# Slot logits in column groups by token tile, with a running maximum and total in each group

## The chip, the cores and the metric

The program runs on one core of one Trainium2 chip. A core has engines that run side by side and meet at semaphores: TensorE (PE in the profile), which multiplies matrices and writes to PSUM, eight banks of 128 partitions x 512 fp32 columns; its weight loader (PEld); VectorE (DVE), ScalarE (ACT) and GpSimd (POOL), which work on PSUM and on SBUF; and SyncE (SP), which issues most transfers (DMA) from and to HBM. The metric is device time in microseconds (us) of one execution, as the median of several runs; lower is better.

## The reference

Three stages in a row, all fp32, on 2304 tokens of width 512. The first is attention with random features (exponentials of projections in place of a softmax), the second a mixture of four experts (`relu(x @ w1[e]) @ w2[e]`, weighted by probabilities that are given). The change lies in the third, a mixture through slots; `x` is the second stage's output, `phi` is 512 x 32:

```
logits = x @ phi                                  # 2304 tokens x 32 slots
d = softmax of logits over the tokens (axis 0)
slot_input = d.T @ x                              # 32 slots x 512
slot_out[e] = relu(slot_input[e] @ w1[e]) @ w2[e] # 8 experts of 4 slots, inner width 1024
c = softmax of logits over the slots (axis 1)
out = c @ slot_out                                # 2304 x 512
```

The first softmax needs the maximum and the total over all tokens, before `slot_input` is final, and every slot waits for all tokens. The kernel does it as a running softmax: each group of tokens is scaled by the maximum so far, and what was summed before is corrected by the factor f = exp(old maximum - new maximum).

## The kernel before

The second stage is the longest. Each product of 128x384 tiles is three matmuls of high and low parts, and the blocks are combined so that seven products do the work of eight. The tokens lie in three buffers `x2[0..2]` of 768 tokens, features on the partitions, four blocks k of 128 features. The last seven second-layer products of the last unit (each 12 matmuls, L784) are P1 to P7 in a string `ENDING` (L841), which is written by hand and gives the order in which the program's pieces are emitted, and so the order on each engine: each engine runs its own instructions in that order and waits at semaphores. Between the products the string puts the first slot tasks; the digit is the group of tokens:

```
"l0 P1 l1 t0 P2 t1 l2 b0 P6 a0 t2 l3 b1 P5 a1 t3 g0 P3 b2 a2 l4 g1 P7 b3 a3 t4 g2 P4 b4 a4 g3"
```

There are NB = 6 groups of three tiles of 128 tokens. For each:

- l, `slot_logits`: four matmuls 32x384 (L956), one for each feature block k. The 32 slots fill only 32 of the array's 128 columns, so block k goes to column group k: partitions 32k to 32k+31 of the PSUM tile `lq` hold the part that block k gives. ScalarE copies `lq` to SBUF (L960; VectorE in the last group).
- t, `slot_sum`: one matmul with `sumr` (L966), a 128x128 matrix of four by four identities of 32, adds the four parts and leaves the sum `lt` on all four groups of partitions. VectorE takes the negative maximum (L974) and the smaller of it and the old one (L975), ScalarE writes the exponentials and their row totals (L978 and the read of the accumulator behind it), copies the plain logits (L981), and computes f (L987).
- b, `slot_back`: three transposes (L1007) of 64 rows, 32 of exponentials and 32 of plain logits, put tokens on the partitions; VectorE copies both out (L1015, L1012).
- a, `slot_turns`: for each tile four transposes of `x` into one bank `tpm` (L943 is the line of the transposes in the profile) and a copy of 128x512 to SBUF (L945).
- g, `slot_gather`: d.T @ x, three matmuls 32x512 (L1025), tile i in column group i, so three partial sums lie below one another in `acc`; VectorE adds them to the running sum, scaled by f (L1036), and brings the total up to date (L994).

PSUM tiles of these tasks take turns in the four banks of the group "s": a fifth tile has to wait until the first has been read for the last time.

What follows the string is the tail: logits, turns, sum and back of the last group, with the gather of the one before. `slots_turn` (L1100) then multiplies the running sum, 96 partitions, with `sf` (`sumr` times f, L1094): that adds the three partial sums and puts features on the partitions (`tps`), and a second time for the last group's own sum, which is first copied out (L1107, L1108). L1111 copies `tps` to `sp`, and `hidden` (L1160) starts the slots' first layer, `second_layer` (L1188) the second. The weights of these layers are 32 tiles of 1 MB; the loop at L1147 issues them from SyncE, and those whose place in SBUF is still in use wait there for the last reader.

Of the kernel before, what the change touches and what calls it, by code (L numbers as in the profile page):

```python
# [16 lines left out]
P = 128  # L17
# [20 lines left out]
NB = NT // NP  # L38
# [7 lines left out]
def body(ctx: ExitStack, tc: tile.TileContext, ql, kl, vl, om, dp, wl, phi, w2l, out):  # L46
# [786 lines left out]
    def widen():  # L833
# [8 lines left out]
        "l0 P1 l1 t0 P2 t1 l2 b0 P6 a0 t2 l3 b1 P5 a1 t3 g0 P3 b2 a2 l4 g1 P7 b3 a3 t4 g2 P4 b4 a4 g3"  # L842
# [68 lines left out]
    def begin_keep():  # L911
        nonlocal keep, lgs
        keep = prep.tile([P, NT + 2 * NP, NS], F32, name="keep", tag="prb0")
        lgs = keep[:, 0:NT]

    keep = lgs = None
# [4 lines left out]
    def slot_task(s):  # L921
        {"l": slot_logits, "t": slot_sum, "a": slot_turns, "b": slot_back, "g": slot_gather}[s[0]](int(s[1]))
# [3 lines left out]
    def spare_place(n):  # L926
        if n not in places:
            if n < 6:
                t = w1e.tile([P, 6, DM], F32, name="mo", tag="w1x")
                places.update({k: t[:, k] for k in range(6)})  # L930
            else:
                tag = ("u1", "u2", "s1", "s2", "u4", "r22")[n - 6]
                places[n] = lt.tile([P, DM], F32, name=f"sp_{tag}", tag=tag)
        return places[n]

    mo = spare_place

    def slot_turn(n, i):
        b, c0 = n // 2, (n % 2) * TH + i * P
        x = spare_place(4 + (n % 2) * 3 + i)  # L940
        tp = bank("s", "tpm").rearrange("p (k t) -> p k t", k=NK)
        for k in range(NK):
            nc.tensor.transpose(tp[:, k, :], x2[b][:, k, c0:c0 + P], ident)  # L943
        copy = nc.vector.tensor_copy if n == NB - 1 and i == 1 else nc.scalar.copy
        copy(out=x, in_=tp.rearrange("p k t -> p (k t)"))  # L945
        st["x2t", n, i] = x

    def slot_turns(n):
        for i in range(NP):
            slot_turn(n, i)  # L950

    def slot_logits(b):
        c0 = (b % 2) * TH
        lq = bank("s", "lq")[:, 0:TH]
        for k in range(NK):
            nc.tensor.matmul(  # L956
                lq[32 * k:32 * k + 32, :], lhsT=phis[:, k, :], rhs=x2[b // 2][:, k, c0:c0 + TH], start=True, stop=True,
            )
        st["lq", b] = mo(1 + 2 * (b % 2))
        (nc.vector.tensor_copy if b == NB - 1 else nc.scalar.copy)(out=st["lq", b][:, 0:TH], in_=lq)  # L960

    def slot_sum(n):

        w = TH
        lt = bank("s", "lt")[:, 0:w]
        nc.tensor.matmul(  # L966
            lt, lhsT=sumr.rearrange("p j s -> p (j s)"), rhs=st["lq", n][:, 0:w], start=True, stop=True
        )
        m, old = mrun[n % 2], mrun[(n + 1) % 2]
        if n == 0:  # L970
            nc.vector.tensor_reduce(out=m, in_=lt, axis=AX.X, op=ALU.max, negate=True)
        else:
            mt = mp.tile([P, 1], F32, name="mt", tag="mt")
            nc.vector.tensor_reduce(out=mt, in_=lt, axis=AX.X, op=ALU.max, negate=True)  # L974
            nc.vector.tensor_tensor(out=m, in0=mt, in1=old, op=ALU.min)  # L975
        st["dt", n] = mo(10) if n % 2 else mo(2)
        ds = tot if n == 0 else mp.tile([P, 1], F32, name="ds", tag="ds", bufs=3)
        nc.scalar.activation(out=st["dt", n][:, 0:w], in_=lt, func=AF.Exp, bias=m, scale=1.0, accum_out=ds)  # L978
        def as_they_are():

            nc.scalar.copy(out=st["dt", n][NS:2 * NS, 0:w], in_=lt[NS:2 * NS])  # L981

        if n < NB - 1:
            as_they_are()
        if n:
            st["f", n] = mp.tile([P, 1], F32, name="f", tag="f", bufs=3)
            nc.scalar.activation(out=st["f", n], in_=old, func=AF.Exp, bias=m, scale=-1.0)  # L987
        if n == NB - 1:
            as_they_are()
        st["ds", n] = ds  # L990

    def slot_total(n):
        if n:
            nc.vector.scalar_tensor_tensor(  # L994
                out=tot, in0=tot, scalar=st["f", n], in1=st["ds", n], op0=ALU.mult, op1=ALU.add
            )

    def slot_back(b):

        nt = NP  # L1000
        d = st["d", b] = keep[:, NT + NP * (b % 2):NT + NP * (b % 2) + NP]
        st["lg", b] = lgs[:, NP * b:NP * b + NP]
        tp = bank("s", "dp")[:, 0:nt * 2 * NS].rearrange("p (i a s) -> p i a s", a=2, s=NS)
        def back(a0, a1):
            r = slice(a0 * NS, a1 * NS)
            for i in range(nt):
                nc.tensor.transpose(  # L1007
                    tp[:, i, a0:a1, :].rearrange("p a s -> p (a s)"), st["dt", b][r, i * P:(i + 1) * P], ident[r, r]
                )

        def logits():
            nc.vector.tensor_copy(out=st["lg", b][:, 0:nt, :], in_=tp[:, :, 1, :])  # L1012

        back(0, 2 if b < NB - 1 else 1)
        nc.vector.tensor_copy(out=d[:, 0:nt, :], in_=tp[:, :, 0, :])  # L1015
        if b < NB - 1:
            logits()
        else:
            st["rest"] = lambda: (back(1, 2), logits())

    def slot_gather1(b):

        acc = bank("s", "acc")
        for i in range(NP):
            nc.tensor.matmul(  # L1025
                acc[32 * i:32 * i + 32, :], lhsT=st["d", b][:, i, :], rhs=st["x2t", b, i], start=True, stop=True,
            )
        return acc[0:NS * NP]

    def slot_gather2(b, acc):  # L1030
        s1 = mo(0)[0:NS * NP]
        if b == 0:
            nc.gpsimd.memset(mo(0)[NS * NP:P], 0.0)
            nc.vector.tensor_copy(out=s1, in_=acc)
        else:
            nc.vector.scalar_tensor_tensor(  # L1036
                out=s1, in0=s1, scalar=st["f", b][0:NS * NP], in1=acc, op0=ALU.mult, op1=ALU.add
            )
        slot_total(b)

    def slot_gather(b):
        slot_gather2(b, slot_gather1(b))
# [43 lines left out]
    nc.gpsimd.memset(s2[NS * NP:P], 0.0)  # L1086
    slot_logits(n)
    slot_turn(n, 0)
    slot_turn(n, 1)
    slot_sum(n)  # L1090
    slot_gather(n - 1)
    slot_turn(n, 2)
    sf = mp.tile([P, NS], F32, name="sf")
    nc.vector.tensor_scalar_mul(sf, sumr[:, 0, :], st["f", n])  # L1094
    slot_back(n)
# [9 lines left out]
    slots_turn(0, mo(0), sf)  # L1105
    acc = slot_gather1(n)
    nc.scalar.copy(out=s2[0:NS * NP, 0:HD], in_=acc[:, 0:HD])  # L1107
    nc.vector.tensor_copy(out=s2[0:NS * NP, HD:DM], in_=acc[:, HD:DM])  # L1108
    slots_turn(1, s2, sumr[:, 0, :])
    st["rest"]()  # L1110
    nc.scalar.copy(out=sp, in_=tp)  # L1111
    slot_total(n)
    nc.vector.tensor_scalar_add(tot, tot, 1e-9)
    nc.vector.reciprocal(out=rtot, in_=tot)
# [213 lines left out]
```

## Time and profile before

| | |
|---|---|
| median of three runs | 958.35 us (957.3 to 959.7) |
| profiled execution | 953.06 us |
| span of its trace | 951.3 us |
| TensorE busy | 932.7 us, 98% of the span |
| VectorE, ScalarE, GpSimd busy | 79%, 45%, 37% |
| first logits matmul of the third stage (L956) | 856.3 us into the span |
| first matmul of the slots' first layer (L1160) | 901.07 us |

The span runs from the first to the last instruction of the trace; the rest of an execution's time, 1.76 us here, lies around it. "Busy" sums an engine's instructions over the span. A view by windows cuts the span into stretches and gives for each engine its busy time, the number of instructions, the clock that TensorE was granted (1.00 is full) and the share of the transfer engines in use. The chain of waits goes back from the last instruction: at each step to what released it, or to the instruction before it on the same engine; what is on it set the end. In the rows, an fp32 matmul of the program appears as two records, so that four matmuls of 128x32 are x8.

### The profile page before, as it was taken

Reading aid. Unit: us, or ns where it says so; the run is one execution under the profiler, and the core shown is the slowest. Engines: PE = TensorE matmul, PEld = TensorE weight load, DVE = VectorE, ACT = ScalarE, POOL = GpSimd, SP = SyncE. Lnnn points to the kernel's source line nnn. Section 1 sums busy time; section 2 is a strip of 40 time slices with the busy share of each in tenths; the row PEclk is TensorE's granted clock in tenths of the full one; section 3 lists DMA queues with packets and bytes.
Section 4 is the critical chain, followed back from the end, with each engine's and each line's share of the span. In section 5 each row is a group of like instructions: output and inputs, shape, how many; then the busy total and the mean of one; then the engine's idle time right before and its main releaser. Section 6 shows DMA issues by size and latency. Waiting matters only on the chain.

```text
span 951.3 us, 15807 instructions
## 1 busy us (share of the span) xinstructions
PE 932.7 (98%) x6065; PEld 888.9 (93%) x6065; DVE 752.3 (79%) x1134; ACT 428.5 (45%) x841; POOL 353.7 (37%) x290
## 2 busy tenths in 40 slices
PE   8999999999999999999999999999999999999997
PEld 7999989999999999999999999999999999997544
DVE  7788885999998878888888888788888888876432
ACT  4899885335543334334244334343342433325322
POOL 7877872432452341434043423414250534000000
PEclk9999999999999999999999999999999999999998
DMA  7678767684968776887767666767667677747897
GB/s 254 220 238 308 246 219 238 193 300 140 350 219 298 242 244 210 303 264 256 247 212 243 211 230 206 253 212 251 210 228 239 216 249 223 272 154 287 354 419 284
DMA packets 82111, 236.51 MB, mean 249 GB/s; under 512 B 8749, under 2 KB 36597, under 8 KB 77941
## 3 DMA queue, kind: packets, MB, share of 16 engines
q1 hardware_dynamic: 78292, 225.29, 69.2%
q10 hardware_dynamic: 3744, 10.23, 2.8%
q8 instruction: 48, 0.79, 0.3%
q14 instruction: 27, 0.21, 0.1%
HBM read 211.86 MB, written 23.63 MB: 248 GB/s over the span
## 4 chain that ended last, share of the span: by engine, by line
PE 86%; DVE 6%; DMA 3%; ACT 2%; issue 1%; SPq 0%; ACTq 0%; DVEq 0%
PE X L608 19%; PE X L784 18%; PE B L608 15%; PE B L784 14%; PE kv L221 3%; PE num L245 3%; PE pj L177 2%; PE so L1188 2%; PE tp L235 2%; PE pj L178 2%; PE pj L179 2%; PE hq L1160 1%; DMA raw<-kl 1%; DVE x L806 1%; DMA x<-xt 1%
## 5 line engine op out<-in xcount | busy, mean ns | idle before, releaser
L806 DVE TENSOR_TENSOR x<-X,x 128x768 f32<-128x768 f32 x84 | 80.0, 952 | 42.0 <-PE X L784 42.0
L419 POOL TENSOR_TENSOR Tw<-raww 128x512 f32<-128x512 f32 x30 | 41.3, 1397 | 192.5 <-DMA raww<-wl 192.5
L608 PE MATMUL X<-x,w1h 128*128 128x384 f32 x432 | 110.2, 335 | 0.2 <-PE B L784 0.2
L608 PE MATMUL B<-x,w1h 128*128 128x384 f32 x432 | 109.9, 335 | 0.0
L608 PE MATMUL X<-x,w1x 128*128 128x384 f32 x504 | 94.2, 334 | 0.6 <-DMA x<-xt 0.6
L608 PEld LDWEIGHTS X<-x,w1x 128*128 128x128 f32 x504 | 87.9, 188 | 0.9 <-ACT u L690 0.9
L202 ACT ACTIVATE fe<-pj,nb 128x128 f32<-128x128 f32 x288 | 82.7, 390 | 8.3 <-DVE nb L195 6.6
L655 ACT CAST s3h<-X 128x768 fp32r<-128x768 f32 x21 | 16.8, 802 | 147.7 <-DVE X L665 138.4
L608 PEld LDWEIGHTS X<-x,w1h 128*128 128x128 f32 x432 | 77.6, 188 | 0.8 <-PE B L784 0.5
L608 PEld LDWEIGHTS B<-x,w1h 128*128 128x128 f32 x432 | 77.8, 188 | 0.0
L608 PE MATMUL B<-x,w1l 128*128 128x384 f32 x216 | 72.2, 334 | 0.0
L608 PE MATMUL X<-x,w1l 128*128 128x384 f32 x216 | 72.2, 334 | 0.0
L806 DVE TENSOR_TENSOR x<-B,x 128x768 f32<-128x768 f32 x72 | 68.3, 949 | 3.3 <-PE B L784 2.8
L438 POOL TENSOR_TENSOR w2l<-raww,w2h 128x512 fp32r<-128x512 f32 x24 | 37.1, 1560 | 80.1 <-ACT w2h L437 80.1
L679 ACT COPY u<-X 128x768 f32<-128x768 f32 x63 | 50.1, 795 | 23.8 <-PE X L608 23.6
L185 DVE TENSOR_REDUCE stat<-pj 128x4 f32<-128x512 f32 x72 | 49.5, 687 | 12.7 <-PE pj L179 11.9
L438 POOL TENSOR_TENSOR w2l<-Tw,w2h 128x512 fp32r<-128x512 f32 x32 | 46.5, 1464 | 30.0 <-ACT w2h L437 30.0
L152 POOL TENSOR_TENSOR lo<-raw,hi 128x512 fp32r<-128x512 f32 x35 | 44.7, 1276 | 21.3 <-ACT hi L149 20.6
L438 POOL TENSOR_TENSOR w1l<-raww,w1h 128x512 fp32r<-128x512 f32 x25 | 38.0, 1524 | 36.6 <-ACT w1h L437 36.6
L655 ACT CAST e11h<-B 128x768 fp32r<-128x768 f32 x21 | 16.8, 801 | 77.0 <-PE B L784 68.5
L438 POOL TENSOR_TENSOR w1x<-Tw,w1x 128x512 fp32r<-128x512 f32 x21 | 27.7, 1317 | 57.4 <-ACT w1x L437 57.4
L608 PE MATMUL B<-x,w1x 128*128 128x384 f32 x252 | 47.1, 334 | 0.2 <-DMA x<-xt 0.2
(260 smaller groups left out, 2749.6 us busy)
## 6 DMA issues: line engine op xcount, KB each, us to landing
x<-xt SPq DMA_DIRECT2D x84, 768.0 KB, 5.3
x<-xd SPq DMA_DIRECT2D x75, 768.0 KB, 4.7
raww<-wl SPq DMA_DIRECT2D x16, 1024.0 KB, 6.8
w2tb<-w2l SPq DMA_DIRECT2D x11, 1024.0 KB, 9.6
raw<-ql SPq DMA_DIRECT2D x18, 512.0 KB, 5.0
xd<-xst SPq DMA_DIRECT2D x36, 256.0 KB, 3.0
prb<-prd SPq DMA_DIRECT2D x23, 384.0 KB, 6.6
raw<-kl SPq DMA_DIRECT2D x16, 512.0 KB, 5.8
```

Source lines behind the costliest of these rows:

```text
L152: (nc.gpsimd if i else nc.vector).tensor_tensor(out=lo, in0=r, in1=f32(hi), op=ALU.subtract)
L185: nc.vector.tensor_reduce(out=stats(i)[:, 4 * g:4 * g + 4, 0], in_=pjs[i, g], axis=AX.X, op=ALU.max)
L202: nc.scalar.activation(out=feats[i][:, 4 * g + h, :], in_=pjs[i, g][:, h, :], func=AF.Exp, bias=biases[i, g][:, h:h + 1], scale=1.0,)
L221: nc.tensor.matmul(kvps[b][h // 4][:, h % 4, :], lhsT=feats[i][p0:p0 + np_, h, :], rhs=v[p0:p0 + np_, h, :], start=first and h % 4 == 0, s ...
L245: nc.tensor.matmul(num[p0:p0 + n, h, :], lhsT=fts[i][:, 4 * g + h, p0:p0 + n], rhs=kvt[b][:, 4 * g + h, :], start=True, stop=True,)
L419: nc.gpsimd.tensor_tensor(out=out_, in0=a, in1=b_, op=op)
L438: nc.gpsimd.tensor_tensor(out=lo, in0=src, in1=f32(hi), op=ALU.subtract)
L608: nc.tensor.matmul(o, lhsT=lhs[:, jp, c], rhs=rhs[:, :, k, :], start=first and not k and not n, stop=False, skip_group_check=True,)
L655: nc.scalar.copy(out=pair(hs[i][0]), in_=src)
L679: nc.scalar.copy(out=pair(tmp({I1: "u1", I6: "u2", I5: "u4"}[i])), in_=q)
L784: nc.tensor.matmul(q[:, c, :], lhsT=lhs[:, jp, cs], rhs=rhs[:, jp, :], start=i in (I1, I2, I7) and jp == 0 and m == 0, stop=False, skip_gr ...
L806: nc.vector.tensor_tensor(out=o, in0=q, in1=o, op=ALU.add)
```

## The change

The tokens are now cut in five groups, `TG`: three of four tiles and two of three. The logits are laid out by tile, not by feature block: tile i of the group has column group i, and its four feature blocks are added up in PSUM in that column group (`start` at the first, `stop` at the last). So `lq` is 128 partitions (tile and slot) x 128 tokens and holds finished logits; the copy to SBUF and the matmul with `sumr`, task t, are gone. Each column group keeps a running maximum and total of its own (`mrun` and `tot` are 128 different values now, before they were four copies of 32). Exponentials and plain logits are both 128x128, and slot_back turns each with one transpose of 128x128. The gather is as before, with four tiles beside each other.

In the tail the four column groups are joined. `apart` spreads the 128 maxima over four columns by a mask, `slots_across` multiplies these with `sumr`, so that each partition sees the four groups' values of its slot, and takes the minimum of the negative maxima (`low`); w = exp(the group's own maximum minus the largest of the four) weights the groups: `s4w` is `sumr` times w, and times f for what was summed before, and `slots_turn` uses it in place of `sf` and `sumr`. The totals are weighted and added by a second `apart` and `slots_across`.

A cut of the diff, unchanged and removed lines left out where they are many:

```diff
...
-NB = NT // NP
+TG = [(0, 4), (4, 4), (8, 4), (12, 3), (15, 3)]
+NB = len(TG)
...
     ENDING = (
-        "l0 P1 l1 t0 P2 t1 l2 b0 P6 a0 t2 l3 b1 P5 a1 t3 g0 P3 b2 a2 l4 g1 P7 b3 a3 t4 g2 P4 b4 a4 g3"
+        "l0 P1 l1 P2 b0 P6 a0 b1 P5 g0 l2 a1 P3 g1 b2 P7 l3 a2 P4 g2 b3 a3"
...
     def begin_keep():
...
+        nonlocal lgs
+        lgs = prep.tile([P, NT, NS], F32, name="lgs", tag="prb0")
+        nc.gpsimd.memset(small(0, 4), 0.0)
+        for i in range(4):
+            nc.gpsimd.memset(small(i, 1)[32 * i:32 * i + 32], 1.0)
+    lgs = None
     tot = mp.tile([P, 1], F32, name="tot")
...
-        {"l": slot_logits, "t": slot_sum, "a": slot_turns, "b": slot_back, "g": slot_gather}[s[0]](int(s[1]))
+        {"l": slot_logits, "a": slot_turns, "b": slot_back, "g": slot_gather}[s[0]](int(s[1]))
     places = {}
...
-                tag = ("u1", "u2", "s1", "s2", "u4", "r22")[n - 6]
+                tag = ("u1", "u2", "u4", "s1", "s2", "r22")[n - 6]
                 places[n] = lt.tile([P, DM], F32, name=f"sp_{tag}", tag=tag)
...
+    def small(c, n):
+        return mo(2)[:, 384 + c:384 + c + n]
+    def slot_tile(n, i):
+        b, r = divmod(TG[n][0] + i, TB)
+        return x2[b], slice(r * P, (r + 1) * P)
     def slot_turn(n, i):
-        b, c0 = n // 2, (n % 2) * TH + i * P
-        x = spare_place(4 + (n % 2) * 3 + i)
+        x = spare_place(3 + 4 * (n % 2) + i)
         tp = bank("s", "tpm").rearrange("p (k t) -> p k t", k=NK)
+        y, c = slot_tile(n, i)
         for k in range(NK):
-            nc.tensor.transpose(tp[:, k, :], x2[b][:, k, c0:c0 + P], ident)
+            nc.tensor.transpose(tp[:, k, :], y[:, k, c], ident)
         copy = nc.vector.tensor_copy if n == NB - 1 and i == 1 else nc.scalar.copy
         copy(out=x, in_=tp.rearrange("p k t -> p (k t)"))
         st["x2t", n, i] = x
     def slot_turns(n):
-        for i in range(NP):
+        for i in range(TG[n][1]):
             slot_turn(n, i)
...
+    def rows(n):
+        return slice(0, NS * TG[n][1])
+    def slot_logits(n):
+        lq = bank("s", "lq")[:, 0:P]
         for k in range(NK):
...
+            for i in range(TG[n][1]):
+                y, c = slot_tile(n, i)
+                nc.tensor.matmul(
+                    lq[32 * i:32 * i + 32, :], lhsT=phis[:, k, :], rhs=y[:, k, c], start=k == 0, stop=k == NK - 1,
+                )
+        r = rows(n)
         m, old = mrun[n % 2], mrun[(n + 1) % 2]
         if n == 0:
-            nc.vector.tensor_reduce(out=m, in_=lt, axis=AX.X, op=ALU.max, negate=True)
+            nc.vector.tensor_reduce(out=m, in_=lq, axis=AX.X, op=ALU.max, negate=True)
         else:
             mt = mp.tile([P, 1], F32, name="mt", tag="mt")
...
+            nc.vector.tensor_reduce(out=mt[r], in_=lq[r], axis=AX.X, op=ALU.max, negate=True)
+            nc.vector.tensor_tensor(out=m[r], in0=mt[r], in1=old[r], op=ALU.min)
+        dt = st["dt", n] = mo(1 + n % 2)
         ds = tot if n == 0 else mp.tile([P, 1], F32, name="ds", tag="ds", bufs=3)
...
+        nc.scalar.activation(out=dt[r, 0:P], in_=lq[r], func=AF.Exp, bias=m[r], scale=1.0, accum_out=ds[r])
         if n:
...
+            f = st["f", n] = mp.tile([P, 1], F32, name="f", tag="f", bufs=3)
+            if n == NB - 1:
+                nc.gpsimd.memset(f[r.stop:P], 1.0)
+            nc.scalar.activation(out=f[r], in_=old[r], func=AF.Exp, bias=m[r], scale=-1.0)
+        nc.scalar.copy(out=dt[r, P:2 * P], in_=lq[r])
         st["ds", n] = ds
     def slot_total(n):
         if n:
+            r = rows(n)
             nc.vector.scalar_tensor_tensor(
-                out=tot, in0=tot, scalar=st["f", n], in1=st["ds", n], op0=ALU.mult, op1=ALU.add
+                out=tot[r], in0=tot[r], scalar=st["f", n][r], in1=st["ds", n][r], op0=ALU.mult, op1=ALU.add
             )
...
+    def slot_back(n):
+        r = rows(n)
+        t0, nt = TG[n]
+        dt = st["dt", n]
+        st["d", n] = dt[:, 2 * P:3 * P].rearrange("p (i s) -> p i s", s=NS)
+        def back(tp, *parts):
+            for a in parts:
+                nc.tensor.transpose(tp[:, a * P:a * P + r.stop], dt[r, a * P:(a + 1) * P], ident[r, r])
+        def logits(tp):
+            nc.vector.tensor_copy(
+                out=lgs[:, t0:t0 + nt, :], in_=tp[:, P:P + r.stop].rearrange("p (i s) -> p i s", s=NS)
+            )
+        def rest():
+            tp = bank("s", "dp")
+            back(tp, 1)
+            logits(tp)
+        tp = bank("s", "dp")
+        back(tp, *((0, 1) if n < NB - 1 else (0,)))
+        nc.vector.tensor_copy(out=dt[:, 2 * P:2 * P + r.stop], in_=tp[:, r])
+        if n < NB - 1:
+            logits(tp)
         else:
...
+            st["rest"] = rest
+    def slot_gather1(n):
...
-    def slot_gather(b):
-        slot_gather2(b, slot_gather1(b))
+        slot_total(n)
+    def slot_gather(n):
+        slot_gather2(n, slot_gather1(n))
+    def apart(c, v):
+        nc.vector.tensor_scalar_mul(small(c, 4), small(0, 4), v)
+    def slots_across(c, op):
+        a = bank("s", "across")[:, 0:4]
+        nc.tensor.matmul(a, lhsT=sumr.rearrange("p j s -> p (j s)"), rhs=small(c, 4), start=True, stop=True)
+        nc.vector.tensor_reduce(out=small(c + 4, 1), in_=a, axis=AX.X, op=op)
+        return small(c + 4, 1)
     def slot_shares():
         mx = mp.tile([P, NT, 1], F32, name="cmx")
     groups.update({"aq": [4], "bq": [5], "a": [2, 3, 0], "b": [1, 4], "c": [5, 6], "d": [7]})
     n = NB - 1
     s2 = mo(11)
-    nc.gpsimd.memset(s2[NS * NP:P], 0.0)
+    nc.gpsimd.memset(s2[rows(n).stop:P], 0.0)
     slot_logits(n)
+    last = mrun[n % 2]
+    apart(8, last)
+    slot_gather(n - 1)
+    low = slots_across(8, ALU.min)
+    w = small(16, 1)
+    nc.scalar.activation(out=w, in_=last, func=AF.Exp, bias=low, scale=-1.0)
+    s4w = mp.tile([P, 2, NS], F32, name="s4w")
+    nc.vector.tensor_scalar_mul(s4w[:, 1, :], sumr[:, 0, :], w)
+    nc.vector.tensor_scalar_mul(s4w[:, 0, :], s4w[:, 1, :], st["f", n])
     slot_turn(n, 0)
     slot_turn(n, 1)
-    slot_sum(n)
-    slot_gather(n - 1)
+    slot_back(n)
     slot_turn(n, 2)
...
+    slot_total(n)
+    nc.vector.tensor_tensor(out=small(17, 1), in0=tot, in1=w, op=ALU.mult)
+    apart(20, small(17, 1))
     tp = bank("bq", "tps")[:, 0:NK * NS].rearrange("p (k s) -> p k s", k=NK)
-    def slots_turn(m, lhs, rhs):
+    def slots_turn(m, lhs):
         for k in range(NK):
             nc.tensor.matmul(
-                tp[:, k, :], lhsT=lhs[:, k * P:(k + 1) * P], rhs=rhs,
+                tp[:, k, :], lhsT=lhs[:, k * P:(k + 1) * P], rhs=s4w[:, m, :],
                 start=m == 0 and k == 0, stop=m == 1, skip_group_check=True,
             )
-    slots_turn(0, mo(0), sf)
+    slots_turn(0, mo(0))
     acc = slot_gather1(n)
...
+    nc.scalar.copy(out=s2[rows(n), 0:HD], in_=acc[:, 0:HD])
+    nc.vector.tensor_copy(out=s2[rows(n), HD:DM], in_=acc[:, HD:DM])
+    total = slots_across(20, ALU.add)
     st["rest"]()
+    slots_turn(1, s2)
     nc.scalar.copy(out=sp, in_=tp)
...
+    nc.vector.tensor_scalar_add(rtot, total, 1e-9)
+    nc.vector.reciprocal(out=rtot, in_=rtot)
     slot_shares()
     for free in (mp, x2p, lt, w2p, hp, w1e, xop, w1p):
```

TensorE, between the first products. In before the logits (lq) of a group are followed, a few pieces later, by their sum (lt), and then by the turn back (dp); tpm are the turns of x, X the expert's product, acc the gather:

```order
L943 MATMUL tpm<-ident,x_0_2996 128x128 x12
L966 MATMUL lt<-mo,sumr 128x384
L956 MATMUL lq<-x_1_3276,phis 32x384 x4
L1007 MATMUL dp<-ident,sp_u_9248 128x64 x3
L784 MATMUL X_9197<-s1h,w2h 128x384
...
L943 MATMUL tpm<-ident,x_0_2996 128x128 x12
L966 MATMUL lt<-mo,sumr 128x384
L1025 MATMUL acc<-mo,keep 32x512 x2
L1025 MATMUL acc<-sp_u_9295,keep 32x512
L784 MATMUL X_9197<-s4h,w2h 128x384
```

After, in the same place:

```order
L953 MATMUL tpm<-ident,x_0_2996 128x128 x16
L1007 MATMUL dp<-ident,mo 128x128 x2
L785 MATMUL X_9216<-s1h,w2h 128x384
...
L1031 MATMUL acc<-mo 32x512 x3
L1031 MATMUL acc<-sp_u_9316,mo 32x512
L970 MATMUL lq<-x_1_3276,phis 32x128 x16
L953 MATMUL tpm<-ident,x_0_2996 128x128 x8
L953 MATMUL tpm<-ident,x_1_3276 128x128 x8
L785 MATMUL X_9216<-s4h,w2h 128x384
```

The lt rows are gone, a logits row counts sixteen matmuls of 128 columns in place of four of 384, a run of turns is four tiles long, and the turn back is two transposes in place of three.

TensorE in the tail, from the last group's logits to the first layer (hq), before:

```order
L956 MATMUL lq<-x_2_3576,phis 32x384 x4
L943 MATMUL tpm<-ident,x_2_3576 128x128 x8
L966 MATMUL lt<-mo,sumr 128x384
L1025 MATMUL acc<-mo,keep 32x512 x2
L1025 MATMUL acc<-sp_u_9295,keep 32x512
L943 MATMUL tpm<-ident,x_2_3576 128x128 x4
L1007 MATMUL dp<-ident,sp_u_9248 128x32 x3
L1100 MATMUL tps<-sf,mo 128x32 x4
L1025 MATMUL acc<-sp_u_9337,keep 32x512
...
L1100 MATMUL tps<-sumr,sp_r_9524 128x32 x4
L1007 MATMUL dp<-ident,sp_u_9248 128x32 x3
L1160 MATMUL hq<-pre_4823,sp 32x512 x4
```

After:

```order
L970 MATMUL lq<-x_2_3576,phis 32x128 x12
L1031 MATMUL acc<-sp_u_9372,mo 32x512
...
L1056 MATMUL across<-mo,sumr 128x4
L953 MATMUL tpm<-ident,x_2_3576 128x128 x8
L1007 MATMUL dp<-ident,mo 128x96
L953 MATMUL tpm<-ident,x_2_3576 128x128 x4
L1124 MATMUL tps<-s4w,mo 128x32 x4
L1031 MATMUL acc<-mo 32x512 x3
L1056 MATMUL across<-mo,sumr 128x4
L1007 MATMUL dp<-ident,mo 128x96
L1124 MATMUL tps<-s4w,sp_r_9531 128x32 x4
L1184 MATMUL hq<-pre_4823,sp 32x512 x4
```

The sum lt between the turns is gone, the gather of the group before stands ahead of the turns and a matmul `across` behind it; a second `across` and the plain logits' turn now stand between the last gather and the second tps.

VectorE in the tail, from the last group's maximum on, before (the first row is the copy of its logits parts):

```order
L960 COPY mo<-lq 128x384
L945 COPY sp_s_9344<-tpm 128x512
L974 TENSOR_REDUCE mt<-lt 128x1
L975 TENSOR_TENSOR mrun_2974<-mt,mrun_2973 128x1
L1036 SCALAR_TENSOR_TENSOR mo<-mo,f,acc 96x512
L994 SCALAR_TENSOR_TENSOR tot<-tot,f,ds 128x1
L1094 TENSOR_SCALAR sf<-sumr,f 128x32
L1015 COPY keep<-dp 128x96
L1108 COPY sp_r_9524<-acc 96x256
L1012 COPY keep<-dp 128x96
```

After:

```order
L979 TENSOR_REDUCE mt<-lq 96x1
L980 TENSOR_TENSOR mrun_2973<-mt,mrun_2974 96x1
L1051 TENSOR_SCALAR mo<-mo,mrun_2973 128x4
L1042 SCALAR_TENSOR_TENSOR mo<-mo,f,acc 96x512
L995 SCALAR_TENSOR_TENSOR tot<-tot,f,ds 96x1
L1057 TENSOR_REDUCE mo<-across 128x1
L1111 TENSOR_SCALAR s4w<-sumr,mo 128x32
L1112 TENSOR_SCALAR s4w<-s4w,f 128x32
L955 COPY mo<-tpm 128x512
L1021 COPY mo<-dp 128x96
L995 SCALAR_TENSOR_TENSOR tot<-tot,f,ds 96x1
```

The copy of lq is gone; the masked spread (L1051) stands behind the maximum, and the reduction of `across` (L1057) and both products for `s4w` behind the sum with the gather (L1042), where one product `sf` stood.

## Rows read from the trace of the kernel before

**Rows 1.** The page: the span, and busy time of each engine

```profile
span 951.3 us, 15807 instructions
...
PE 932.7 (98%) x6065; PEld 888.9 (93%) x6065; DVE 752.3 (79%) x1134; ACT 428.5 (45%) x841; POOL 353.7 (37%) x290
```

**Rows 2.** Windows: stretch, sum; PE, PEld, DVE, ACT, POOL busy; clock, DMA share, GB/s

```profile
856.28:868.26 11.98, 11.87 (x77) 8.53 (x76) 9.76 (x16) 7.10 (x15) 0.00 (x0) 1.00 0.92 357
868.26:889.60 21.34, 21.34 (x138) 15.02 (x138) 10.17 (x23) 11.38 (x26) 0.52 (x1) 1.00 0.62 231
889.60:901.07 11.47, 10.54 (x78) 6.30 (x78) 5.65 (x15) 4.69 (x11) 1.85 (x2) 1.00 1.01 424
901.07:925.00 23.93, 23.93 (x250) 10.03 (x254) 9.28 (x46) 6.16 (x10) 0.00 (x0) 1.00 1.01 419
```

**Rows 3.** Chain of waits between products: start, duration, engine, output, line, records

```profile
868.91 0.65 PE lt L966 x2
869.56 0.78 PE lq L956 x8
870.35 0.33 PE dp L1007 x3
870.67 2.31 PE X L784 x12
872.98 1.31 PE tpm L943 x12
...
874.94 0.99 PE acc L1025 x6
```

**Rows 4.** One line's matmuls: count, ns min/median/max, first and last start, shape

```profile
L956 PE MATMUL lq<-x,phis x48: 486/486/510, 856.3 to 892.6; 128*32 128x384 f32 x48
...
L1100 PE MATMUL tps<-sf,mo x8: 268/276/276, 897.0 to 897.8; 128*128 128x32 f32 x8
```

**Rows 5.** Chain of waits, from the tail into the two slot layers

```profile
896.60 0.13 DVE tot L994
...
897.03 1.05 PE tps L1100 x8
898.08 1.05 PE acc L1025 x6
...
899.15 0.38 ACT sp_r L1107
...
900.75 0.27 ACT sp L1111
...
901.07 7.07 PE hq L1160 x64
...
924.20 4.02 PE so L1188 x72
```

**Rows 6.** One line's instructions on ScalarE and VectorE

```profile
L202 ACT ACTIVATE fe<-pj,nb x288: 357/378/488, 8.7 to 151.7; 128x128 f32<-128x128 f32 x144
...
L978 ACT ACTIVATION_READ_ACCUMULATOR mo<-lt,mrun x3: 192/193/193, 863.9 to 887.7; 128x1 f32 x3
...
L987 ACT ACTIVATE f<-mrun,mrun x5: 282/294/295, 867.4 to 896.3; 128x1 f32<-128x1 f32 x5
...
L1015 DVE COPY keep<-dp x6: 247/250/258, 865.7 to 896.8; 128x96 f32<-128x96 f32 x6
...
L960 DVE COPY mo<-lq x1: 547/547/547, 893.3 to 893.3; 128x384 f32<-128x384 f32 x1
```

**Rows 7.** The last weight tile: its matmuls, its issue, its landing

```profile
L1188 PE MATMUL so<-w2t__9680,ht x16: 379/379/379, 938.5 to 939.2; 128*32 128x256 f32 x16
L1147 SPq DMA_DIRECT2D w2t__9680<-w2l x1: 328/328/328, 914.3 to 914.3; - x1
...
DMA to landing us min/median/max: 20.1/20.1/20.1
```

**Rows 8.** SyncE's waits from 840 us: sum, times, longest

```profile
SPq L1147 <- PE tpm L943: 19.5, 2, 10.1
```

More of the change, by code (lines that the diff above doesn't have):

```diff
@@ L911, in begin_keep @@
     def begin_keep():
[L912 to L916, printed above, removed]
+        nonlocal lgs
[4 more added lines that the diff above has]
+    lgs = None
     tot = mp.tile([P, 1], F32, name="tot")
@@ L948, in slot_turns @@
     def slot_turns(n):
-        for i in range(NP):
+        for i in range(TG[n][1]):
             slot_turn(n, i)
-    def slot_logits(b):
-        c0 = (b % 2) * TH
-        lq = bank("s", "lq")[:, 0:TH]
+    def rows(n):
+        return slice(0, NS * TG[n][1])
+    def slot_logits(n):
+        lq = bank("s", "lq")[:, 0:P]
         for k in range(NK):
[L956 to L968, printed above, removed]
+            for i in range(TG[n][1]):
[4 more added lines that the diff above has]
+        r = rows(n)
         m, old = mrun[n % 2], mrun[(n + 1) % 2]
@@ L970, in slot_sum @@
         if n == 0:
-            nc.vector.tensor_reduce(out=m, in_=lt, axis=AX.X, op=ALU.max, negate=True)
+            nc.vector.tensor_reduce(out=m, in_=lq, axis=AX.X, op=ALU.max, negate=True)
         else:
             mt = mp.tile([P, 1], F32, name="mt", tag="mt")
-            nc.vector.tensor_reduce(out=mt, in_=lt, axis=AX.X, op=ALU.max, negate=True)
-            nc.vector.tensor_tensor(out=m, in0=mt, in1=old, op=ALU.min)
-        st["dt", n] = mo(10) if n % 2 else mo(2)
+            nc.vector.tensor_reduce(out=mt[r], in_=lq[r], axis=AX.X, op=ALU.max, negate=True)
@@ L977, in slot_sum @@
+            nc.vector.tensor_tensor(out=m[r], in0=mt[r], in1=old[r], op=ALU.min)
+        dt = st["dt", n] = mo(1 + n % 2)
         ds = tot if n == 0 else mp.tile([P, 1], F32, name="ds", tag="ds", bufs=3)
[L978 to L984, printed above, removed]
-        if n:
-            st["f", n] = mp.tile([P, 1], F32, name="f", tag="f", bufs=3)
-            nc.scalar.activation(out=st["f", n], in_=old, func=AF.Exp, bias=m, scale=-1.0)
@@ L988, in slot_sum @@
-        if n == NB - 1:
-            as_they_are()
+        nc.scalar.activation(out=dt[r, 0:P], in_=lq[r], func=AF.Exp, bias=m[r], scale=1.0, accum_out=ds[r])
+        if n:
+            f = st["f", n] = mp.tile([P, 1], F32, name="f", tag="f", bufs=3)
[3 more added lines that the diff above has]
+        nc.scalar.copy(out=dt[r, P:2 * P], in_=lq[r])
         st["ds", n] = ds
@@ L993, in slot_total @@
         if n:
+            r = rows(n)
             nc.vector.scalar_tensor_tensor(
-                out=tot, in0=tot, scalar=st["f", n], in1=st["ds", n], op0=ALU.mult, op1=ALU.add
+                out=tot[r], in0=tot[r], scalar=st["f", n][r], in1=st["ds", n][r], op0=ALU.mult, op1=ALU.add
             )
[L998 to L1017, printed above, removed]
-        else:
-            st["rest"] = lambda: (back(1, 2), logits())
@@ L1021, in slot_gather1 @@
-    def slot_gather1(b):
+    def slot_back(n):
[19 more added lines that the diff above has]
+            logits(tp)
+        else:
+            st["rest"] = rest
@@ L1023, in slot_gather1 @@
+    def slot_gather1(n):
         acc = bank("s", "acc")
-        for i in range(NP):
+        for i in range(TG[n][1]):
             nc.tensor.matmul(
-                acc[32 * i:32 * i + 32, :], lhsT=st["d", b][:, i, :], rhs=st["x2t", b, i], start=True, stop=True,
+                acc[32 * i:32 * i + 32, :], lhsT=st["d", n][:, i, :], rhs=st["x2t", n, i], start=True, stop=True,
             )
[L1028 to L1033, printed above, removed]
+        return acc[rows(n)]
@@ L1034, in slot_gather2 @@
+    def slot_gather2(n, acc):
+        r = rows(n)
+        s1 = mo(0)[r]
+        if n == 0:
             nc.vector.tensor_copy(out=s1, in_=acc)
@@ L1036, in slot_gather2 @@
             nc.vector.scalar_tensor_tensor(
-                out=s1, in0=s1, scalar=st["f", b][0:NS * NP], in1=acc, op0=ALU.mult, op1=ALU.add
+                out=s1, in0=s1, scalar=st["f", n][r], in1=acc, op0=ALU.mult, op1=ALU.add
             )
-        slot_total(b)
-    def slot_gather(b):
-        slot_gather2(b, slot_gather1(b))
+        slot_total(n)
[8 more added lines that the diff above has]
+        return small(c + 4, 1)
     def slot_shares():
```

9 lines of the change are left out of this document (removed).

## The prediction

> **What bounds the kernel now.** I read the page first: TensorE is busy for 932.7 of 951.3 us [rows 1], so a saving counts only if it takes time off TensorE, or off a wait in its order. Then the windows around the third stage's first part, from the first logits matmul at 856.28 to the first layer of the slots at 901.07: 44.79 us. There TensorE is busy for 11.87 + 21.34 + 10.54 = 43.75 us at the full clock [rows 2]; VectorE and ScalarE are at half their time. 1.04 us are idle, and 0.93 of them in the tail (889.60 to 901.07). Third, the chain of waits: between the products it runs along TensorE without a break, row after row (sum, logits, turn back, product, turns) [rows 3]. So this part is a list of TensorE work, and the change can be told as a ledger: what is struck off, what is put on, what becomes idle. Last, the weights: behind 901.07 the windows show the transfer engines full at 419 GB/s [rows 2], so I had to see whether a first layer that starts sooner still finds its weights.
>
> **The ledger of TensorE work.**
>
> *Struck off.* Six sums lt of 0.65 us [rows 3]: -3.9. One gather of six: five groups cost the same 0.99 to 1.05 each [rows 3, 5], since four tiles lie beside each other where three did: -0.95. The turn back: three transposes take 0.33 [rows 3], and there are six such and one more in the tail's end (the last group's plain logits), 2.3 in all. A transpose of 128x128 takes 1.31/12 = 0.11 [rows 3], and a change from one kind of matmul to another costs 0.115 (worked out below, at the logits); so four pairs at 0.22 + 0.115 = 0.33 and two single ones at 0.22, 1.8 in all: -0.5. The 72 transposes of x stay; one run of them less saves one change of kind: -0.1.
>
> *Put on: the logits.* This is the term with the least support, since the trace has no matmuls of 128 columns in four column groups. It has the same form at three other widths. Sixty-four records of 512 columns, in sixteen sets of four, take 7.07 us; seventy-two records of 256 columns, in eighteen sets, take 4.02 [rows 5]. That is 0.442 and 0.223 a set, so 0.219/256 = 0.855 ns a column and 0.004 us a set that no column pays for. At 384 columns this gives 0.332 a set; two sets make 0.66, and the logits row shows 0.78 [rows 3], so 0.115 goes to the change of kind. At 128 columns: 0.114 a set. The after kernel's four feature blocks are eight sets (two records for each matmul): 8 x 0.114 + 0.115 = 1.03 a group, in the groups of three tiles too, since a column group's stream is as long. Five groups are 5.15 where six were 6 x 0.78 = 4.68: +0.47. From below, the columns alone would be 8 x 0.109 = 0.88 (+0.1 on the ledger with the change of kind); from above, a set can't be told to be shorter than the nearest that was seen, 0.223, which gives 1.90 a group. I take 1.03: two widths on a line through zero, and a third that fits.
>
> *Put on: the joining.* Two matmuls `across` of four columns. Nearest is tps with 32 columns, eight records in 1.05 that last 0.276 each [rows 4, 5]: (1.05 - 0.276)/7 = 0.11 apart. Two records are 0.22 each time; were one to wait for the other, 0.55. I take 0.2: +0.4.
>
> Together -3.9 - 0.95 - 0.5 - 0.1 + 0.47 + 0.4 = -4.6 us of busy time.
>
> **The idle time.** Before, 1.04 us, of which 0.53 lies ahead of the second tps (the last gather ends at 899.13, `sp_r` is copied for 0.38 from 899.15, and tps, 1.05 long, must have begun at 899.7 to let `sp` start at 900.75), and 0.3 behind it (the copy `sp`, 0.27) [rows 5]. The copy of `sp` stays. The 0.53 are mostly filled: the second `across` and the last turn back (0.2 + 0.2) stand there now, leaving 0.1.
>
> New is a wait at PSUM's banks. The "s" tiles take turns in four banks, so the fifth tile behind a group's logits needs their bank back. Ahead of a run of four turns this is its fourth tile: `lq`, three turns, then the fourth turn in `lq`'s own bank. It is free only when ScalarE has made the last read of `lq`, the plain copy, which stands behind maximum, minimum, exponential, accumulator and f. A VectorE read of PSUM takes 0.250 at 96 columns and 0.547 at 384 [rows 6], so 0.28 at 128; the minimum 0.13 (as a one-column operation, [rows 5]); the exponential of 128x128 0.38, the accumulator 0.19, f 0.29 [rows 6]; the copy 0.27 (as `sp`, 128x128, [rows 5]). That is 1.54, with hand-overs between engines (0.02 to 0.14, read off the gaps of [rows 5]) about 1.85. Three turns cover 3 x 0.44 + 0.1 = 1.4. So 0.45 us of TensorE's time is lost in the runs behind l2 and l3; queued behind the waiting turn are the product P3 or P4 and all else. l0 and l1 have a product of 2.31 behind them, which covers it; in the tail the gather, `across` and a turn come first (1.0 + 0.2 + 0.5), about even. Stalls: 0.9, plus 0.1 ahead of `across`. Bounds: 0 if ScalarE and VectorE are quick, 1.8 if each is twice as long.
>
> Idle after: 0.9 + 0.1 + 0.1 + 0.3 = 1.4, so +0.35 against 1.04.
>
> **Covered, at no cost.** w and `s4w`: from the last logits' end, maximum and minimum 0.4, the spread 0.2, then VectorE's queue: the sum with the gather of the group before has to pass (0.7 behind the gather's end), then the reduction 0.2, w on ScalarE 0.3, two products 0.4; with hand-overs 3 us (estimates between the 0.13 of one column and the 0.25 of 96 [rows 5, 6]). TensorE has the gather, `across`, three turns and the turn back in that time, 1.0 + 0.2 + 1.4 + 0.2 = 2.8 to 3.0. This cover is just long enough; every 0.1 that the chain is longer costs 0.1. GpSimd's small fills have nothing in their way. The plain logits' copy grew from 32x384 to 128x128 and the copy of `lq` (0.47 a group) is gone, both on engines that are half idle [rows 2].
>
> **The weights.** The last tile is issued at 914.25, lands 20.1 later at 934.3, and is first used at 938.5 [rows 7]: 4.2 us of slack. If nothing moved it, a first layer 4.3 us sooner would just meet it, and cap the gain at 4.2. But the stream as a whole is held up by SyncE's wait for a transpose of x, 10.1 us long [rows 8], the turns of a2 now, which end some 2 us sooner. I count nothing.
>
> **Sum.** -4.6 + 0.35 = -4.25: the first layer starts at about 896.8, and what follows moves with it. The profiled execution was 953.06, 1.76 more than its span; it would be 948.8. It lies 5.3 under the median of the runs, so I carry over the difference, not the time: 958.35 - 4.3 = **954.0 us**.
>
> **The rivals.** (A) *A narrow set is not shorter than a wider one*: each record has a price of its own, and 128 columns go by at 0.223 a set, as 256 do. Then a group is 1.90, +0.87 five times = +4.35, and the gain is gone: 958.3. For it: no row is narrower in this form, and tps' records, with 32 columns only, still come 0.11 apart, so a record of that form has a floor. Against it: 0.004 us a set is all that the two widths leave for such a price. 9%. The Trainium skill, TensorEngine Tiling (Array Packing), section Performance Considerations under Instruction Overhead, says that each matmul carries about 60 cycles and that one shouldn't take the tiling factor from a dimension that is already small; that is what this change does with the tokens, 384 to 128. At 2.4 GHz 60 cycles are 0.025 us, an estimate from that page: four records of a set make 0.1, less than 0.114 if they overlap, and rival A's time if they add up.
>
> (B), *slower*: each set adds to the same PSUM columns as the set before it. If it waited for that one's result, a set would take a record's whole length. A logits record lasts 0.486 [rows 4] against 0.332 of streaming, so 0.154 more: 0.114 + 0.154 = 0.268 a set, 2.26 a group, +1.23 five times = +6.2, and 960.2. It turns to a loss from 0.114 + 4.3/40 = 0.22 a set. Against it: the two records of one logits matmul add to the same columns too, and the second starts before the first one's 0.486 are over, or 0.78 would not do for both. 4%.
>
> (C) *The new waits are not covered*: the bank stalls are longer, or the joining chain is late at tps. Three places at 0.5 to 0.9 more: a gain of 1.5 to 2.8, 955.6 to 956.9. For it: three dependent chains over three engines, whose hand-overs I have from few rows. 21%.
>
> (D) *The weights hide part*: the stream stays where it was and the first layer's earlier reads don't help; a gain of 3 to 4.2, 954.2 to 955.4. 6%.
>
> **How the numbers follow.** The forecast (all covered but the two stalls) has 60%, and its own range is 952.8 (no stalls: -5.2, and 0.3 of the runs' scatter) to 955.3. Less than 0.3%, 2.9 us, can't be told from no change here. Faster takes the forecast but for 0.01, D but for 0.01, and 0.05 of C: 0.69. Same takes most of C, A but for 0.01, and those: 0.26. Slower is B and that little of A: 0.05. The range for 8 in 10 takes in the forecast, D and C, with scatter on either side: 952.0 to 957.8.
>
> **What would show it.** A logits row of 1.0 us with 32 records, and no lt; 1.9 or 2.3 would be A or B. The product P4 beginning at about 883.5 by the same prices. Two idle stretches of 0.45 ahead of a run's fourth turn, released by ScalarE's plain copy. The first layer at 896.8, with less than 0.2 of idle time ahead of the first tps. The last weight tile landing at 932 to 934 ahead of its use at 934.2. I am wrong if the part from the first logits to the first layer isn't 40 to 41 us, or if it is and the end doesn't follow it.

## The result and the profile after

The changed kernel takes 950.59 us, median of six runs (948.06 to 952.14), against 958.18 for the kernel before (six runs): a ratio of 0.9916, 95% interval 0.99 to 0.9932, so 6.5 to 9.6 us less. The forecast was 954.0 and the range 952.0 to 957.8: the sign was right, the gain almost twice what was forecast. Two executions far off all others stay out of what follows: the first one of the version with 128-row extra transposes (1858.5 us, the granted clock given as 1.00) and one of twelve of the version with filled gaps (3267.5 us).

The profiled execution took 952.14 us, little less than that of before. Its page:

```profile
span 950.4 us, 15968 instructions
...
PE 931.5 (98%) x6142; PEld 894.7 (94%) x6142; DVE 751.3 (79%) x1133; ACT 421.9 (44%) x833; POOL 354.5 (37%) x295
...
PEclk9799999999999999999999999999999999999998
```

The third row is the clock granted to TensorE in 40 slices of 24 us, in tenths: the second slice is at 7, where before showed 9 there. By windows (columns as in [rows 2]; the stretches are the ten microseconds ahead of that dip, the dip, then the part of the third stage from the first logits to the first layer, cut where the product P4 begins):

```profile
20.00:30.00 10.00, 8.79 (x73) 8.24 (x71) 8.07 (x26) 6.16 (x21) 9.52 (x10) 1.00 0.41 151
30.00:42.00 12.00, 11.78 (x59) 11.06 (x58) 5.23 (x16) 7.84 (x26) 6.24 (x7) 0.57 0.52 183
861.50:887.43 25.93, 25.79 (x264) 22.03 (x264) 17.11 (x31) 10.74 (x29) 0.61 (x2) 1.00 0.80 318
887.43:900.16 12.73, 12.00 (x105) 8.51 (x104) 7.02 (x24) 5.56 (x15) 0.53 (x1) 1.00 0.93 371
```

For 12 us the granted clock was 0.57 in the mean, between TensorE's two levels, 2.4 and 1.2 GHz; in the ten microseconds ahead of it the engine had been idle for 1.2. So the first logits came at 861.5 in this execution and at 856.3 in the other. This is not the change's doing: in a later execution of the changed kernel that has no such dip they came at 857.1. So traces must be compared from the first logits on. There the part takes 38.7 us in place of 44.79 [rows 2], 6.1 less (forecast 40.5); P4 starts 25.9 after its beginning (forecast 27.2). What follows the first layer's start is 50.2 us long in both.

The chain of waits after (start, duration, engine, output, line, records), between the products and in the tail:

```profile
862.57 2.30 PE X L785 x12
864.87 1.01 PE lq L970 x32
...
870.51 1.75 PE tpm L953 x16
872.26 0.22 PE dp L1007 x2
872.48 2.11 PE X L785 x12
874.59 0.99 PE acc L1031 x8
875.58 0.88 PE lq L970 x32
876.46 0.60 PE tpm L953 x4
...
877.98 0.66 PE tpm L953 x4
...
894.26 0.36 PE across L1056 x2
894.62 0.93 PE tpm L953 x8
...
896.09 1.08 PE tps L1124 x8
...
898.75 1.06 PE tps L1124 x8
...
900.16 7.07 PE hq L1184 x64
```

Set beside [rows 3], three things are to be seen. A logits row has 32 records and takes 1.01, as forecast. No lt stands in it. And the turn back dp takes 0.22, and the product behind it 2.11, where before they were 0.33 and 2.31; a product behind logits still takes 2.30. The fourth turn waits, at 877.98 as foreseen (0.60 + 0.66 of turns in a stretch of 2.17). The logits' records last 0.273 each and yet 32 go by in 1.01:

```profile
L970 PE MATMUL lq<-x,phis x144: 272/273/298, 861.5 to 892.9; 128*32 128x128 f32 x144
```

The last weight tile is issued at 916.0 and first used at 937.6:

```profile
L1212 PE MATMUL so<-w2t__9701,ht x16: 378/379/380, 937.6 to 938.3; 128*32 128x256 f32 x16
L1171 SPq DMA_DIRECT2D w2t__9701<-w2l x1: 328/328/328, 916.0 to 916.0; - x1
...
DMA to landing us min/median/max: 19.8/19.8/19.8
```

### The profile page after: what moved, and what is told of

It is laid out like the page before. It is cut to its first block, busy times and chain, and to the rows that moved or that the text cites. A ratio compares the mean times of both kernels' runs of the same rounds, so it can differ in the third digit from the quotient of the medians.

```text
span 950.4 us, 15968 instructions
## 1 busy us (share of the span) xinstructions
PE 931.5 (98%) x6142; PEld 894.7 (94%) x6142; DVE 751.3 (79%) x1133; ACT 421.9 (44%) x833; POOL 354.5 (37%) x295
## 4 chain that ended last, share of the span: by engine, by line
PE 85%; DVE 7%; DMA 3%; ACT 2%; issue 2%; SPq 0%; ACTq 0%; DVEq 0%
PE X L785 18%; PE X L609 18%; PE B L609 14%; PE B L785 14%; PE kv L222 3%; PE num L246 3%; PE pj L178 2%; PE so L1212 2%; PE tp L236 2%; PE pj L179 2%; PE pj L180 2%; PE hq L1184 1%; DMA xt<-xr 1%; DVE x L807 1%; DMA raw<-kl 1%
## 5 line engine op out<-in xcount | busy, mean ns | idle before, releaser
L153 POOL TENSOR_TENSOR lo<-raw,hi 128x512 fp32r<-128x512 f32 x35 | 44.7, 1277 | 26.1 <-ACT hi L150 25.5
L178 PE MATMUL pj<-om_hi,hi 128*128 128x256 f32 x144 | 46.5, 323 | 2.3 <-ACT fe L203 2.3
```

Of the source, the lines that this page charges most:

```text
L153: (nc.gpsimd if i else nc.vector).tensor_tensor(out=lo, in0=r, in1=f32(hi), op=ALU.subtract)
L178: nc.tensor.matmul(o, lhsT=hi[:, pi, :], rhs=om_hi, start=True, stop=False)
```

## The experiments

What is compared below is the part from the first logits to the first layer in the trace of each version. It repeats well: 44.76 to 44.79 us in five traces of before, 38.62 to 38.67 in three of after.

The first question was why the product behind dp had become shorter. *Theory 1*: TensorE pays when the cut of its array changes, that is, how many rows x columns of it a matmul takes up (128x128 for products, turns and lt; 128x32 for logits and gather; 64x128 for the turn back of before), and not for a change of work in the same cut. *Theory 2*, the prediction's: the price belongs to every change of kind.

**The turn back of before over all 128 rows.**

```diff
-    st["dt", b][r, i * P:(i + 1) * P], ident[r, r]     # r: 64 rows, 32 in the last group
+    st["dt", b][:, i * P:(i + 1) * P], ident
```

> The kernel before, with one edit: the turn back transposes all 128 partitions of each token tile (the other copies of the slots are turned too and not read), where it took 64 rows (32 in the last group). Theory 1 (TensorE pays when the cut of its array changes, 128x128 to 64x128 or 128x32 and back, and not for another kind of work in the same cut): a transpose is longer by 0.05, but behind it the next product takes 2.11 in place of 2.31 and the next turns 1.31 in place of 1.46, and no cut changes ahead of it where a product or turns stand there; about 0.1 us less for each of six groups, so the part from the first logits to the first layer goes from 44.8 to about 44.1. Theory 2 (the price belongs to the change of kind, as the prediction had it): nothing saved, six times three longer transposes, 0.8 more: 45.6.

Measured: 44.7 in place of 44.8, near neither number. The chain shows why:

```profile
879.89 0.33 PE dp L1006 x3
880.22 1.31 PE tpm L943 x12
...
896.76 0.17 DVE mrun L975
...
897.84 0.48 ACT sp_u L981
...
898.36 0.55 PE dp L1006 x3
```

Between the products the rows are theory 1's: dp stays at 0.33 though each transpose is wider, and the turns behind it take 1.31, not 1.46. Up to the last turn the part is 39.0 long where before had 39.5: 0.5 less. But the last dp reads all rows now, the plain logits among them, and so waits for ScalarE's plain copy, which ends at 898.32: the wait takes the 0.5 back. As a test of the price it speaks for theory 1, as a sum it failed, through a wait that I had not foreseen.

**Extra transposes inside the products**, two in each of the last unit's seven, 14 in all, first of 64 rows, then of 128:

```diff
+    if u == NU - 1 and jp == 0:
+        nc.tensor.transpose(acc2[key][:, c, TH:TH + 64], ident[0:64], ident[0:64, 0:64])
```

> The changed kernel with two added transposes of 64 rows of the identity inside each of the last unit's seven products (14 in all), into unused columns of the product's own bank; nothing reads them. Theory 1: each costs a change of cut on the way in and one on the way out beside its own 0.06: 0.3 to 0.4, 14 of them 4.2 to 5.6 us in the part from the first logits to the first layer (38.6 before the edit). Theory 2 (a change of kind costs 0.115 each way whatever the cut): 0.3 each, 4.1 in all, and the same with 128 rows.

> The changed kernel with 14 added transposes of all 128 rows of the identity inside the last unit's products, two in each, as with the 64-row ones. Theory 1 (the price belongs to a change of the array's cut): none here, 0.11 to 0.15 each for 128 columns, 1.5 to 2.1 us on the part from the first logits to the first layer (38.7 without them), where the 64-row ones, half the work, took 5.6. Theory 2 (a change of kind costs 0.115 each way): 0.34 each, 4.8 us.

Measured: the part is 44.2 with 64 rows and 40.2 with 128, against 38.7: 5.6 us and 1.5 us, 0.40 and 0.107 each. The chains, first with 64 rows (L790 is the extra transpose), then with 128:

```profile
868.70 1.01 PE lq L972 x32
869.72 0.72 PE B L785 x3
870.44 0.20 PE B L790
870.64 1.25 PE B L785 x6
```

```profile
861.65 1.01 PE lq L972 x32
862.66 0.73 PE B L785 x3
863.39 0.11 PE B L790
863.50 1.07 PE B L785 x6
```

Half the columns cost four times as much. A transpose of 64 columns would be 0.05 by itself, half of the 0.107 (an estimate), so a change of cut and back costs 0.35, or 0.17 for one. In the rows it stands in two places: in the transpose (0.20, not 0.11) and, for the larger part, in the matmuls behind it, which are in the old cut again (1.25 for six, not 1.07). Theory 2 falls: in the same cut a change of work costs nothing that shows. (The extra transposes alter the products' sums; only times are read here.) The Trainium skill, TensorEngine Tiling (Array Packing), section Tiling Modes under Key Properties, has the rule: "Changing tiling mode (not just tile) drains the TensorE". The trace agrees, with 0.17 us here.

**The stalls filled**: l2 ahead of g0, and g1 behind l3.

```diff
-"l0 P1 l1 P2 b0 P6 a0 b1 P5 g0 l2 a1 P3 g1 b2 P7 l3 a2 P4 g2 b3 a3"
+"l0 P1 l1 P2 b0 P6 a0 b1 P5 l2 g0 a1 P3 b2 P7 l3 g1 a2 P4 g2 b3 a3"
```

> The changed kernel with two moves in the string: l2 ahead of g0, and g1 behind l3, so that a gather stands between the logits and the turns whose fourth tile waits for the logits' bank. The prediction's stall (0.42 and 0.41 in the trace after): both go, 0.8 us less, the part from first logits to first layer 38.6 to 37.8. Rival: the wait moves on to the third turn or to the turn back, and less than 0.3 is won.

The part is 37.8, 0.9 less, and the turns stand in one piece:

```profile
873.39 0.86 PE acc L1031 x8
874.25 1.90 PE tpm L953 x16
876.14 2.11 PE X L785 x12
```

As a number this is what was expected, but the two moves also took out two changes of cut. At 0.1 to 0.17 each, the prices of the other runs, these are 0.2 to 0.3 of it (an estimate), and the stalls 0.6. Timed, it is 0.9913 of before (0.9882 to 0.9943).

**Fewer changes of cut.** In the same string l0 and l1 ahead of P1, and g2 last, next to the tail's logits.

> As the one with the stalls filled, and the tasks in the cut of 32 columns put next to each other: l0 and l1 ahead of P1, and g2 last, ahead of the tail's l4 and g3. Theory 1: two pairs of changes of cut fewer, 0.1 and 0.2 each, 0.6 us less beside the 0.8: the part 37.2. Theory 2: the same 0.4 to 0.5, since these are changes of kind as well. Rival: the weights' last transfer, which in the trace after lands 2 us ahead of its use, or a copy that comes late, takes it back: no better than the stalls filled.

The part is 37.4: 0.4 less, not 0.6, for four changes between 128x128 and 128x32, so 0.1 each; the run of logits l0 l1 is 1.88 where it was 2 x 1.01 and a cut. 0.9911 of before (0.988 to 0.9942).

**One cut in the tail too**: dp of the two short groups over all 128 partitions (`dt[:, a * P:(a + 1) * P], ident`).

> As the one with fewer cuts, and the turn back of the two groups of three tiles over all 128 partitions too (the last 32 hold an earlier group's values, and what they give is not read). Theory 1: between the tail's turns no change of cut is left (before and behind the plain 96-row transposes), four fewer at about 0.1: the part from first logits to first layer 37.4 to 37.0. Theory 2: nothing, or 0.1 more for the wider transposes.

A miss: the part is 37.4 again, though by theory 1's count six changes of cut are gone. Two of the six lie ahead of the tail, where TensorE waits for nothing. The rows there, first with 96 rows (the version with fewer changes), then with 128:

```profile
885.23 0.17 PE dp L1007 x2
885.40 1.31 PE tpm L953 x12
```

```profile
888.18 0.22 PE dp L1007 x2
888.40 1.31 PE tpm L953 x12
```

The turns take 1.31 behind either, where behind a 64-row dp they took 1.46, and with 96 rows dp itself is shorter, 0.17 in place of 0.22. So a transpose of 96 rows between work of 128 is no change of cut that costs: what the expectation counted was never paid, in the tail or ahead of it. Theory 1 holds for 64 rows and for 32 columns, and 96 rows are counted as 128 from here on. Timed, it is 0.9888 of before (0.9859 to 0.9917), the best measured; the changed kernel beside it was at 0.9896, so this isn't a difference.

**Why the medians moved more than the part.** 6.1 us of 7.6 are in the part. I ran both kernels again.

> The kernel before, unchanged, as a control for the early part. The profiled executions say that the change saves 6.2 us between the first logits and the first layer, the timed medians 7.6. If the rest is chance (TensorE's clock granted at half speed for some 10 us near 30 us into the span in some executions and not in others), the ratio to itself is 1 within 0.003 and the times differ by several us with the granted clock. If the rest belongs to the change, the times of before stay above 957 at any clock.

> The changed kernel, unchanged, on the same chip. If 6.2 us is the gain, 0.9935 of before with an interval that holds it; if 7.6 or more, 0.992 or lower and an interval that leaves 0.9935 out.

> The changed kernel again, on another occasion, to see whether the 1.4 us by which the timed medians moved more than the traced part is there again: at equal granted clock 6.2 below before (0.9935), with more only if its executions are again less throttled than those of before. If the change itself makes for less throttling, the mean granted clock of its runs is above that of before here too, by 0.0015 or more; if it was chance, the two are alike.

Before to itself: 1.0007 (0.9981 to 1.0034), times from 953.43 to 965.0. After: 0.9912 (0.9882 to 0.9942), an interval that holds 0.9935 and 0.992 alike, and, on the third occasion, 0.9896 (0.9871 to 0.9921), which leaves 0.9935 out. In 74 runs of before and 21 of after, the time falls along a straight line in the granted clock (by some 0.86 us for 0.001), and at equal clock after is 6.4 us faster, plus or minus 0.5: the part. The rest is clock: 0.9944 in the mean before, 0.9962 after, a difference of 0.0018, three times its uncertainty if the runs count as independent, which is 1.5 us. So it was there again, and chance alone explains it badly. Where does the clock fall? In the trace of the control it did at the first layer's start, behind the tail's gaps:

```profile
900.00:902.00 2.00, 1.58 (x15) 1.43 (x19) 0.67 (x3) 0.48 (x2) 0.82 (x1) 0.90 1.02 426
902.00:904.00 2.00, 2.00 (x12) 0.40 (x8) 1.86 (x6) 0.00 (x1) 0.00 (x0) 0.50 1.01 422
904.00:906.00 2.00, 2.00 (x20) 0.47 (x16) 1.20 (x3) 0.68 (x1) 0.00 (x0) 0.74 1.02 426
```

At 1.2 GHz for some 3 us the first layer takes 1.6 longer. But the trace of the changed kernel with its stalls filled shows the same behind its own tail, where the first layer starts at 897.1:

```profile
898.00:900.00 2.00, 2.00 (x16) 0.54 (x12) 1.24 (x4) 0.62 (x1) 0.39 (x1) 0.50 1.04 434
```

Three more executions of before and a version with the tail's gaps filled (12 matmuls of no use ahead of the first tps, the second, and behind it) were to tell.

> The kernel before, one execution more, to see where TensorE's clock falls. Theory C (the change itself makes for less throttling, at the first layer's start): of four such executions at least two show the clock at half speed right behind the tail's idle gaps, near 902 us, for a loss of 1.7 us each. Theory D (chance): as often as in the changed kernel.

> The kernel before with twelve matmuls of no use (128x256, 0.11 us each) in the tail's three gaps: three ahead of the first tps, six ahead of the second, three behind it. Theory C: with no gap ahead of the first layer the clock no longer falls there, the mean granted clock of its runs rises from 0.9942 to 0.996, and the median falls by 1 to 1.5 us although the fillers may cost 0.3. Theory D: the clock is as before, and the time the same or 0.3 us longer.

None of the three shows the clock low ahead of the last few microseconds; with the first trace and the control that is one in five at the first layer's start, against one in eight of the changed kernel and its versions. The traces of after had their dips at 24 to 42 us (two of three) and, like three of before's five, in the last microseconds. With the gaps filled: 0.9991 (0.9971 to 1.0011) and a part of 45.3, so the fillers cost 0.5; the mean clock of eleven runs is 0.9955, between the two. Theory C is not shown, theory D not either: that the changed kernel is throttled less is measured, why stays open.

## Why the prediction was wrong

By classes of TensorE's work, from start to start of the matmuls in the part (us; "idle" is the time in which no matmul ran, 0.14 of it after in the stalls):

| | before | after | measured | predicted |
|---|---|---|---|---|
| sums lt | 4.21 | 0 | -4.2 | -3.9 |
| gathers | 5.46 | 4.92 | -0.5 | -0.95 |
| turn back and products | 18.38 | 16.91 | -1.5 | -0.5 |
| turns of x with their stalls | 8.71 | 8.54 | -0.2 | +0.8 |
| logits | 5.03 | 4.91 | -0.1 | +0.47 |
| across | 0 | 0.46 | +0.5 | +0.4 |
| tps | 1.96 | 2.06 | +0.1 | 0 |
| idle | 1.04 | 0.87 | -0.2 | -0.5 (the stalls stand with the turns) |
| sum | 44.8 | 38.7 | -6.1 | -4.2 |

- **The turn back: the step that failed.** "A change from one kind of matmul to another costs 0.115": it is the cut that costs, about 0.17 a time for a cut of 64 rows. I charged the new dp, 128x128 like the products, with a change of kind, and left the products and turns at what they were; so the 0.2 a product and 0.15 a run of turns that the 64-row transposes had cost behind them were never on the ledger. The records of the part have 31 changes of cut before and 16 after; the 14 that lead into or out of 64 or 32 rows are all gone. At 0.17 these are some 2 us (an estimate), of which the ledger had 0.6 at most. The table agrees: without the stalls, which were 0.55, turn back, products and turns fell by 2.2 where 0.6 was forecast, and that 1.6 is most of the 1.9 that were missing. The other misses, 0.1 to 0.4 each, nearly cancel. The price could have been read from the trace of before: turns behind a product took 1.31 [rows 3], turns behind a 64-row dp 1.46.

```profile
878.23 0.33 PE dp L1007 x3
878.56 1.46 PE tpm L943 x12
```

- **The stalls: mechanism right, size off.** They are where they were put, at the fourth turn behind l2 and l3, and ScalarE's plain copy ends them. But a run of four turns takes 2.0 where it takes 1.72 to 1.75 unhindered: 0.28 each, 0.55 in all, against 0.9. I had added the durations of ScalarE's four instructions end to end, 1.13; on record they are 1.09 together, but each starts before the one ahead of it is over, and all four pass in 0.79, from 877.13 to 877.92:

```profile
877.13 0.37 ACT L983 ACTIVATE mo<-lq,mrun 128x128 f32<-128x128 f32 x1 [3.81 <-PE tpm L953]
...
877.67 0.25 ACT L989 COPY mo<-lq 128x128 f32<-128x128 f32 x1
```

- **The logits: right.** 1.01 against 1.03 a group, from two wider rows; A and B would have shown 1.9 and 2.3. The class came out below the forecast as the old logits rows were not all 0.78: they took 5.03 in all, not 4.68. In before's last group the records of logits and gather stand among one another, so the two classes are best read together: 0.7 less, forecast 0.5.
- **The joining chain: covered**, as forecast: tps starts within 0.2 of the last turn's end. C didn't happen.
- **The weights**: the last tile is used 21.6 us after its issue, 19.8 of them until it has landed; D didn't happen. The stream did not stay where it was: the last issue comes 54.5 us behind the first logits, before 58.0.
- **The median.** I carried the difference over from one execution to the median as if the clock were the same. It wasn't, for some 1.5 us more, unexplained.

## What to carry to other kernels

Write the cut of the array beside each row of TensorE's order, and count where it changes: such a change cost 0.17 us here to 64 rows, 0.1 to 32 columns and nothing that shows to 96 rows. It shows mostly in the matmul behind it and can outweigh the work itself, so a transpose over rows that nobody needs can be the cheaper one. What is saved ahead of a wait can be lost in it, as the 0.5 of the first experiment were. And compare traces from the point where the change begins: an execution's own clock moved these totals by more than the change did.

## What the runs showed of the hardware

Streaming in four column groups is proportional down to 128 columns: 0.442 us a set of four records at 512 columns, 0.223 at 256, and 0.11 at 128, where each record lasts 0.273 and the sets accumulate in the same columns. No price for a set shows; I had held one of 0.1 possible.
